# A new order table for the attention, its constants in another order, and TensorE products of the identity at launch and in gaps

## The chip, the cores and the metric

The kernel runs on one core of one Trainium2 chip. The metric is the device time of one execution in microseconds (us), lower is better. Engines: TensorE (PE; its weight loads are listed as PEld), VectorE (DVE), ScalarE (ACT), GpSimd (POOL) and SyncE (SP), which here issues almost all DMAs. Each engine works through its own queue in order and waits on semaphores of the others.

## The reference

An attention with a bias that depends on positions, then two gated feed-forward blocks; all in float32.

```
# q, k, v: (2 batches, 8 heads, 576 positions, 64); hidden = 32
scores = q @ k^T / 8
x    = log1p(|i - j|) / log1p(max(i, 1))
bias = relu(x * w1 + b1) @ w2                 # one table per head
attn = softmax(scores + bias);  a = attn @ v  # (1152 rows, 512)
h = a @ w_in;  g = h * clip(h + 3, 0, 6) / 6;  x = g @ w_out     # 2048 wide
xn = rmsnorm(x) * rms_g
out = (silu(xn @ w_gate) * (xn @ w_val)) @ w_out2                # 1536 wide
```

## The kernel before, in words

**Bias.** The bias of position i is needed for all distances. It is made in 36 groups of 16 positions, four tiles each. For each of the four tiles, one engine makes R (L346 to L356): the table T of log1p(distance), scaled once by w1 (L557), is cut off at a value of the row, NB1 on VectorE or SC on ScalarE (both from the norm table and b1, L558 and L559). START (for the first eight groups) and MID (for the others, in turn) say which engine makes each of the four. Four products with W2b on TensorE (`bias_mm`, token B.n) sum over the hidden units. The result is copied out of PSUM in two parts, scaled by INV (`bias_evac`), and stored to DRAM (`biasd`, L398) in a layout from which a load with another pitch (`bias<-biasd`, L424) reads the sheared bias of 128 query rows. Five such tables, one for each block c of query rows, are written; the first needed is c = 2 (groups 16 to 23). A load of bias waits for all stores of its table.

**Attention.** There are nine tiles of 128 query rows, and four pairs of heads in each: 36 units u. For unit u, token S.u is the scores (L439) into two PSUM buffers, of which there are only two in all. VectorE adds the bias and takes the maximum (L452, once for each head; a second small instruction reads the maximum). ScalarE takes the exponential (L463). TensorE transposes the 9 blocks (T.u.0 with four, T.u.1 with four, T.u.2 with one that holds columns of both heads) into three PSUM buffers shared with the bias products, VectorE or ScalarE copies them out (`et`, L483; ET says which), and PV.u multiplies with v (L501). Keys and queries are loaded (L295, L290, L283) and transposed (kT, qT; copies to kS and q). Raw key blocks have three buffers, so the load of a later block waits until an earlier one was transposed. Every four units the row sums are turned (rps) and copied (rt, L525) and the result is scaled.

**Order.** Each step has a key, a number from PARAMS. Steps with a key below `man` are written out by key for all engines. After that, TensorE follows ORDER, the table of tokens, word for word, while a scheduler places the other engines' instructions and the DMAs. TensorE's queue is in order: a token that waits holds all that follow. SP's queue of DMAs is in order too.

**Feed-forward.** From L713 on, products of split float32 (three passes each, `first` L720 and `second` L765), with weights loaded and split on the way (L124 to L165). The first eight weights are loaded and split during the attention.

Of the kernel before, what the change touches and what calls it, by code (L numbers as in the profile page):

```python
# [18 lines left out]
def shape_tables():  # L19
# [19 lines left out]
ORDER = """
kT.0,0,0 B.16 B.17 B.23 B.20 B.13 B.22 S.0 B.18 kT.0,1,0 B.12 B.9 kT.0,2,0 B.11 qT.0 B.19 B.10 kT.0,0,1 B.8 B.21 qT.1  # L40
kT.0,1,1 kT.1,0,1 T.0.2 S.1 B.14 T.0.0 S.2 kT.1,0,0 T.0.1 T.1.1 S.3 kT.1,1,0 S.4 T.1.2 T.2.2 kT.1,1,1 T.1.0 B.15 T.2.1
T.2.0 PV.0 B.24 B.26 T.3.2 PV.1 S.5 PV.2 T.4.1 T.3.0 B.25 qT.2 rps.0 T.3.1 T.4.0 B.27 T.5.0 T.4.2 S.6 B.28 PV.3 S.7
PV.4 T.5.2 T.5.1 T.6.2 S.8 T.7.0 T.6.1 PV.5 qT.3 T.6.0 S.9 PV.6 T.7.2 B.29 B.30 T.8.0 rps.1 T.8.2 T.7.1 S.10 T.8.1
B.32 B.31 PV.7 T.9.0 T.9.2 S.11 T.10.2 PV.8 T.10.0 B.33 T.9.1 S.12 qT.4 T.10.1 T.11.2 S.13 PV.9 B.35 T.12.0 T.11.0
B.34 PV.10 T.11.1 T.12.2 S.14 PV.11 B.0 rps.2 T.13.0 T.13.1 T.12.1 S.15 T.13.2 T.14.0 B.2 B.1 PV.12 T.14.2 T.14.1 S.16
PV.13 B.3 T.15.0 T.16.0 B.4 qT.5 S.17 T.15.2 T.15.1 rps.3 T.16.2 S.18 B.5 PV.15 PV.14 T.17.1 T.16.1 T.17.0 T.17.2 S.19
T.18.0 B.7 PV.16 PV.17 T.19.0 T.18.2 B.6 S.20 qT.6 T.19.1 T.19.2 S.21 T.18.1 T.20.0 rps.4 S.22 T.20.1 T.20.2 PV.18
PV.19 T.21.2 T.21.0 S.23 PV.20 T.21.1 T.22.1 T.22.0 S.24 PV.21 T.22.2 qT.7 T.23.0 S.25 T.23.2 T.24.2 T.24.0 T.23.1
rps.5 S.26 PV.22 PV.23 T.24.1 S.27 T.25.0 T.26.0 T.25.1 T.25.2 PV.24 S.28 T.26.2 T.27.1 qT.8 T.27.2 S.29 PV.25 T.27.0
rps.6 T.26.1 T.28.0 T.28.2 S.30 PV.26 PV.27 T.29.2 T.28.1 T.29.0 S.31 T.30.2 T.30.0 T.29.1 PV.28 T.31.0 S.32 PV.29  # L50
T.30.1 T.31.2 T.31.1 rps.7 PV.31 T.32.2 T.32.1 S.33 PV.30 T.32.0 S.34 T.33.0 T.33.2 T.33.1 S.35 PV.32 T.34.0 T.34.2
# [13 lines left out]
def kernel(ctx, tc, q, k, v, w1, b1, w2, w_in, w_out, w_gate, w_val, w_out2, rms_g, dtab, ntab, itab, out):  # L65
    nc = tc.nc
    B, H, S, D = q.shape
# [168 lines left out]
    if True:  # L236
# [48 lines left out]
        def load_k(b, blk, hh):  # L285

            if blk == 2:
                a = rawp.tile([128, H, D], F32, tag="rawk", name="rawk", bufs=BUFS["rawk"])
                for o in range(2):
                    nc.sync.dma_start(out=a[64 * o:64 * o + 64], in_=rows(k[o, :, 512:576, :]))  # L290
            else:
                a = rawp.tile([128, 2, 4, D], F32, tag="rawk", name="rawk", bufs=BUFS["rawk"])
                for c in range(2):
                    r0 = 256 * blk + 128 * c
                    nc.sync.dma_start(out=a[:, c], in_=rows(k[b, 4 * hh:4 * hh + 4, r0:r0 + 128, :]))  # L295
                a = a.rearrange("p c h d -> p (c h) d")
            raw_t["k", b, blk, hh] = a
# [187 lines left out]
        pv_t = {}  # L485
# [61 lines left out]
        nc.sync.dma_start(out=w2s, in_=w2)  # L547
        load_k(0, 0, 0)
        load_k(0, 1, 0)
        nc.sync.dma_start(out=INV, in_=itab.rearrange("g (o t) -> g o t", o=1).to_broadcast([16, 8, NG]))  # L550

        nc.vector.memset(nb1, 0.0)
        nc.scalar.activation(out=nb1, in_=nb1, func=ACTF.Exp)
        make_identity(nc, ident)
        nc.gpsimd.memset(W2b, 0.0)

        nc.vector.tensor_scalar_mul(T, T, w1c)  # L557
        nc.vector.tensor_scalar(out=NB1, in0=SC, scalar1=b1c, scalar2=-1.0, op0=ALU.mult, op1=ALU.mult)  # L558
        nc.vector.tensor_scalar_mul(SC, SC, b1c)  # L559
# [372 lines left out]
```

## Time and profile before

| what | value |
|---|---|
| median of the runs (three) | 640.93 us (640.75 to 642.7) |
| the profiled execution, its own time | 641.35 us |
| its span, first to last instruction | 639.5 us |
| TensorE busy | 617.6 us, 97% |
| VectorE, ScalarE, GpSimd busy | 442.9, 356.8, 143.6 us |
| chain that ended last, by engine | PE 91%, DMA 3%, DVE 3%, ACT 2% |

The span is what the trace covers; times of rows are counted from its start. A busy share over the whole span hides where an engine idles, so rows are read by stretch. In a row of the trace, "[2.11 <-X]" is the engine's idle time before the row, and what ended it.

### The profile page before, as it was taken

To read this page: it belongs to the slowest core of one execution; us is meant where nothing else is said; L and a number is where in the kernel's file an instruction comes from. 1 tells how busy PE (TensorE), PEld (TensorE's weight loads), DVE (VectorE), ACT (ScalarE), POOL (GpSimd) and SP (SyncE) were. 2 spreads that over 40 slices of the span, in tenths; PEclk is the share of its full clock that TensorE was granted. 3 is DMA by queue.
4 is the path that set the end of the run, shared out by engine and by line. 5 is a ranking of instruction groups with operands and counts; after the bars stand their busy time and mean duration, and the time that the engine had idled before them with its cause. 6 is when DMAs were issued, how large, how long until landed. Compare 5 with 4: busy or idle time off the path is not lost.

```text
span 639.5 us, 10867 instructions
## 1 busy us (share of the span) xinstructions
PE 617.6 (97%) x4136; PEld 520.1 (81%) x4136; DVE 442.9 (69%) x813; ACT 356.8 (56%) x730; POOL 143.6 (22%) x114
## 2 busy tenths in 40 slices
PE   5779999999999999999999999999999999999997
PEld 2246656667878999999999899999899999999996
DVE  5476796647555999888824799979677761387812
ACT  5879888968756555555425455563544331254411
POOL 1000110022110443333300133423323330032400
PEclk9989999999999999999999999999999999999999
DMA  7999867448100343433410133433424340054301
GB/s 161 248 297 266 245 207 209 131 103 205 62 2 1 120 145 133 130 116 120 130 33 1 58 99 121 152 99 118 146 100 132 119 145 2 33 197 135 98 1 49
DMA packets 73953, 77.78 MB, mean 122 GB/s; under 512 B 31917, under 2 KB 58669, under 8 KB 73901
## 3 DMA queue, kind: packets, MB, share of 16 engines
q1 hardware_dynamic: 73636, 77.02, 40.8%
q8 instruction: 32, 0.52, 0.3%
q14 instruction: 21, 0.16, 0.1%
q10 hardware_dynamic: 264, 0.07, 0.0%
HBM read 63.83 MB, written 13.25 MB: 121 GB/s over the span
## 4 chain that ended last, share of the span: by engine, by line
PE 91%; DMA 3%; DVE 3%; ACT 2%; issue 0%; ACTq 0%; SPq 0%; DVEq 0%
PE h L720 39%; PE ya L765 18%; PE yb L765 9%; PE s L439 7%; PE pv L501 7%; PE tps L100 6%; PE bps L369 4%; DVE R L356 1%; DMA biasd<-ev 1%; DMA bias<-biasd 1%; DMA raw<-in_moe_w_out_dram 1%; DMA b1c<-in_b_dram 1%; DVE e L452 1%; PE xnT L100 1%; ACT ev L392 1%; ACT e L463 1%
## 5 line engine op out<-in xcount | busy, mean ns | idle before, releaser
L165 POOL TENSOR_TENSOR wl<-wm,wh 128x512 fp32r<-128x512 f32 x85 | 125.9, 1481 | 302.3 <-ACT wh L136 181.9
L157 DVE SCALAR_TENSOR_TENSOR wm<-raw,wm 128x512 int32<-128x512 int32 x85 | 121.6, 1430 | 1.0
L729 ACT CAST gh<-r 128x384 fp32r<-128x384 f32 x84 | 43.2, 514 | 115.5 <-DVE r L752 68.7
L720 PE MATMUL h<-nh,wh 128*128 128x384 f32 x288 | 97.2, 338 | 0.0
L720 PE MATMUL h<-nh,wl 128*128 128x384 f32 x288 | 96.7, 336 | 0.0
L720 PE MATMUL h<-nl,wh 128*128 128x384 f32 x288 | 96.5, 335 | 0.0
L452 DVE CUSTOM_DVE_ANT_0 e<-s,bias 128x576 f32<-128x576 f32 x72 | 52.0, 754 | 28.1 <-PE s L439 20.1
L720 PE MATMUL h<-xh,wh 128*128 128x384 f32 x192 | 65.4, 340 | 0.0
L720 PE MATMUL h<-xh,wl 128*128 128x384 f32 x192 | 64.7, 337 | 0.0
L720 PE MATMUL h<-xl,wh 128*128 128x384 f32 x192 | 64.5, 336 | 0.0
L463 ACT ACTIVATE e<-e,m 128x576 f32<-128x576 f32 x72 | 55.6, 774 | 14.8 <-DVE m L452 14.6
L752 DVE TENSOR_TENSOR r<-r,h 128x384 f32<-128x384 f32 x36 | 19.9, 551 | 63.3 <-PE h L720 63.3
L153 DVE SCALAR_TENSOR_TENSOR wm<-raw,wm 128x512 int32<-128x512 int32 x85 | 58.9, 693 | 2.8
L732 DVE TENSOR_TENSOR gl<-r,gh 128x384 fp32r<-128x384 f32 x84 | 46.5, 554 | 16.8 <-ACT gh L729 16.8
L144 ACT ACTIVATE wm<-raw 128x512 f32<-128x512 f32 x85 | 57.0, 672 | 2.0 <-DMA raw<-in_moe_w_in_dram 1.5
L720 PEld LDWEIGHTS h<-nh,wh 128*128 128x128 f32 x288 | 54.1, 188 | 2.3 <-DVE nl L829 0.9
L720 PEld LDWEIGHTS h<-nl,wh 128*128 128x128 f32 x288 | 54.1, 188 | 1.4
L720 PEld LDWEIGHTS h<-nh,wl 128*128 128x128 f32 x288 | 54.0, 188 | 0.0
L748 ACT ACTIVATE r<-h 128x384 f32<-128x384 f32 x36 | 17.7, 492 | 64.9 <-PE h L720 64.9
L740 ACT ACTIVATE r<-h,half_c 128x384 f32<-128x384 f32 x48 | 27.7, 577 | 47.0 <-PE h L720 46.8
L136 ACT CAST wh<-wm 128x512 fp32r<-128x512 f32 x85 | 52.3, 616 | 0.9 <-DVE wm L157 0.8
L100 PE MATMUL tps<-ident,e 128*128 128x128 f32 x324 | 48.5, 284 | 2.6 <-DVE R L356 2.1
(95 smaller groups left out, 1101.3 us busy)
## 6 DMA issues: line engine op xcount, KB each, us to landing
raw<-in_moe_w_out_dram SPq DMA_DIRECT2D x33, 512.0 KB, 3.6
biasd<-ev SPq DMA_DIRECT2D x36, 295.5 KB, 4.0
raw<-in_moe_w_in_dram SPq DMA_DIRECT2D x18, 512.0 KB, 3.6
raw<-in_moe_w_gate_dram SPq DMA_DIRECT2D x18, 512.0 KB, 3.5
bias<-biasd SPq DMA_DIRECT2D x15, 576.0 KB, 5.6
raw<-in_moe_w_val_dram SPq DMA_DIRECT2D x16, 512.0 KB, 3.5
bias<-biasd SPq DMA_DIRECT2D x10, 288.0 KB, 5.1
rawk<-in_k_dram SPq DMA_DIRECT2D x18, 128.0 KB, 4.6
```

The lines of the kernel that those rows point to most:

```text
L100: nc.tensor.transpose(out, in_, ident[:n, :n])
L136: nc.scalar.copy(out=hi, in_=m)
L144: nc.scalar.activation(out=m, in_=raw[:, :, 1].bitcast(F32), func=ACTF.Abs, scale=2.0 ** -112)
L153: nc.vector.scalar_tensor_tensor(out=m, in0=raw[:, :, 0], scalar=29, in1=m, op0=ALU.logical_shift_right, op1=ALU.bitwise_or,)
L157: nc.vector.scalar_tensor_tensor(out=m, in0=raw[:, :, 1], scalar=-0x80000000, in1=m, op0=ALU.bitwise_and, op1=ALU.bitwise_or,)
L165: nc.gpsimd.tensor_tensor(out=lo, in0=m, in1=hi, op=ALU.subtract)
L439: nc.tensor.matmul(ps_of["s", u, a][sl, z, :SH], lhsT=q_t[t][half, p, sl], rhs=kS[b][half, p, z * SH:z * SH + SH], start=True, stop=True,)
L452: nc.vector.tensor_tensor_reduce(out=e_t[u][:, a, :].rearrange("p (z j) -> p z j", z=2), in0=s[:, :, :SH], in1=bt[u][:, a, :].rearrange("p ...
L463: nc.scalar.activation(out=e_t[u][:, a, :], in_=e_t[u][:, a, :], func=ACTF.Exp, scale=-1.0, bias=m_t[t][:, h:h + 1], accum_out=sum_t[t][:, ...
L720: nc.tensor.matmul(ps, lhsT=w[wz][:, c * 128:(c + 1) * 128], rhs=x[xz][:, c, :], start=(i == 0), stop=(i == 11),)
L732: nc.vector.tensor_tensor(out=gl, in0=g, in1=gh, op=ALU.subtract)
L765: nc.tensor.matmul(y_t[ph, n, t], lhsT=g[gz][:, t * 128:(t + 1) * 128], rhs=w[wz], start=(f == 0 and i == 0), stop=(f == F - 1 and i == 2),)
```

## The change

The table ORDER, the numbers in PARAMS and the engine strings are new. The constants stand in a block whose order is kept as written, with the loads of b1 and of the norm table exchanged and T scaled ahead of NB1 (in before, the scheduler placed T last). TensorE multiplies the identity by itself: EARLY = 10 times at launch, and twice for each token W, but only while no product with v is being gathered (`pv_t` is empty); that leaves eight of the W tokens with work, 16 products. These results are read by nobody. The last line of the table is shown in the diff; its starts are shown as rows below.

```diff
-    g0=-6.008, gs=0.583, g8=-0.495, gt=-0.138, g14=1.165, gr=1.195, man=-0.96, zra=-1.638, zrd=-0.49, zrp=-1.321,
+    g0=-5.852, gs=0.6, g8=-0.055, gt=-0.219, g14=1.366, gr=1.195, man=-0.96, zra=-1.514, zrd=-0.574, zrp=-2.014,
...
 ORDER = """
...
-T.34.1 PV.33 T.35.2 T.35.1 T.35.0 PV.34 PV.35 rps.8
+T.32.1 T.33.1 S.35 T.34.1 T.33.2 PV.32 PV.33 T.35.1 T.34.2 T.35.0 T.34.0 rps.8 T.35.2 PV.35 PV.34
...
-START = ["DAAA", "DDDD", "DDDD", "DDDD", "DDDD", "DDAA", "DDDD", "DDDD"]
-MID = ["DDAA", "DDDA"]
-ET = ["DADA", "DAAA", "ADAD"]
+START = ["DAAA", "DDDA", "DDDA", "DDDD", "DDDA", "DDDA", "DDDD", "DDDD"]
+MID = ["DDDD", "DDDA"]
+ET = ["DAAA", "AAAD", "DDAD"]
 KE = ["D", "A"]
-RB, RT, XH, XL = "PAAP"
+RB, RT, XH, XL = "PDAP"
+EARLY = 10
...
-        nc.sync.dma_start(out=T, in_=dtab.to_broadcast([128, S]))
-        nc.scalar.dma_start(out=SC, in_=ntab.rearrange("g (o t) -> g o t", o=1).to_broadcast([4, 32, 4 * NG]))
-        nc.sync.dma_start(out=w1c, in_=w1.rearrange("o (k z) -> o k z", z=1).to_broadcast([4, 32, 1]))
-        nc.scalar.dma_start(out=b1c, in_=b1.rearrange("(o k z) -> o k z", o=1, z=1).to_broadcast([4, 32, 1]))
...
+        warm_t = ps_v.tile([128, 4, 128], F32, tag="v", name="warm")
+
+        def warm(n):
+
+            if not pv_t:
+                for z in range(n):
+                    nc.tensor.matmul(warm_t[:, z % 4, :], lhsT=ident, rhs=ident, start=True, stop=True)
+
+        with tc.manual_schedule():
+            nc.sync.dma_start(out=T, in_=dtab.to_broadcast([128, S]))
+            nc.scalar.dma_start(out=b1c, in_=b1.rearrange("(o k z) -> o k z", o=1, z=1).to_broadcast([4, 32, 1]))
+            nc.sync.dma_start(out=w1c, in_=w1.rearrange("o (k z) -> o k z", z=1).to_broadcast([4, 32, 1]))
+            nc.scalar.dma_start(out=SC, in_=ntab.rearrange("g (o t) -> g o t", o=1).to_broadcast([4, 32, 4 * NG]))
...
+            make_identity(nc, ident)
+            nc.gpsimd.memset(W2b, 0.0)
+            warm(EARLY)
+
+            nc.vector.tensor_scalar_mul(T, T, w1c)
+            nc.vector.tensor_scalar(out=NB1, in0=SC, scalar1=b1c, scalar2=-1.0, op0=ALU.mult, op1=ALU.mult)
+            nc.vector.tensor_scalar_mul(SC, SC, b1c)
...
+        for i in range(ORDER.split().count("W")):
+            at(P["man"] + .001 * i, ("W", i), (), warm, 2)
```

Loads and stores on SP's queue, from the query loads to the first bias table's fourth store (rawk, rawq and vs are loads of keys, queries and values; biasd_72 is the first table). Before:

```order
L283 DMA rawq<-in_q_dram 128x8x64 x2
L398 DMA biasd_72<-ev 16x8x591
L304 DMA vs_138<-in_v_dram 128x4x64
L398 DMA biasd_72<-ev 16x8x591 x2
L304 DMA vs_138<-in_v_dram 128x4x64
L398 DMA biasd_72<-ev 16x8x591
```

With the change:

```order
L284 DMA rawq<-in_q_dram 128x8x64 x2
L305 DMA vs_138<-in_v_dram 128x4x64 x2
L399 DMA biasd_72<-ev 16x8x591 x2
L296 DMA rawk<-in_k_dram 128x4x64 x2
L399 DMA biasd_72<-ev 16x8x591 x3
```

Both value loads stand ahead of the first store, and two key loads follow the second store.

TensorE's queue from the second to the third scores (kps, qps and tps are transpositions of keys, queries and exponentials; s is scores; bps is a bias product; kS_136 is the first batch). Before:

```order
L100 MATMUL tps<-ident,e 128x128
L439 MATMUL s<-kS_136,q 128x288 x4
L369 MATMUL bps<-R,W2b 32x352 x4
L100 MATMUL tps<-ident,e 128x128 x4
L439 MATMUL s<-kS_136,q 128x288 x4
```

With the change:

```order
L550 MATMUL warm<-ident 128x128 x2
L440 MATMUL s<-kS_136,q 128x288 x4
L101 MATMUL qps<-ident,rawq 128x128 x4
L550 MATMUL warm<-ident 128x128 x2
L101 MATMUL kps<-ident,rawk 128x128 x4
L101 MATMUL tps<-ident,e 128x128 x4
L440 MATMUL s<-kS_136,q 128x288 x4
L370 MATMUL bps<-R,W2b 32x352 x4
L101 MATMUL tps<-ident,e 128x128
```

The single transposition now stands behind the third scores, and a key block stands ahead of them.

## Rows read from the trace of the kernel before

**Rows 1.** Busy time by stretch: start:end, length, then each engine, clock, DMA share, GB/s.

```profile
6.29:28.40 22.11, 17.82 (x126) 6.52 (x128) 15.99 (x48) 17.27 (x37) 0.94 (x3) 1.00 0.91 220
28.40:45.55 17.15, 12.96 (x86) 7.31 (x80) 11.79 (x31) 15.75 (x37) 0.00 (x0) 0.90 1.04 297
45.55:203.49 157.94, 155.53 (x1699) 109.67 (x1700) 102.38 (x267) 125.15 (x281) 19.24 (x19) 1.00 0.53 148
203.49:639.50 436.01, 431.31 (x2235) 396.59 (x2233) 311.88 (x465) 197.15 (x375) 122.06 (x82) 1.00 0.32 100
```

**Rows 2.** The chain of waits up to 46 us: start, length, what.

```profile
1.92 4.01 DMA b1c<-in_b_dram
...
23.44 4.88 DMA biasd<-ev
...
28.80 4.61 DMA bias<-biasd
...
33.43 0.76 DVE e L452
...
44.89 0.61 DVE kS L328
```

**Rows 3.** TensorE's timeline from 5 to 60 us: start, length, instructions.

```profile
11.45 1.24 PE L369 MATMUL bps<-R,W2b 128*32 128x304 f32 x8 [0.52 <-DVE R L356]
...
13.76 0.74 PE L369 MATMUL bps<-R,W2b 128*32 128x320 f32 x8
...
35.15 0.33 PE L100 MATMUL tps<-ident,e 128*128 128x128 f32 x1 [2.11 <-DVE R L356]
35.41 1.24 PE L439 MATMUL s<-kS,q 64*128 64x288 f32 x8
36.58 1.40 PE L369 MATMUL bps<-R,W2b 128*32 128x352 f32 x8
37.92 1.12 PE L100 MATMUL tps<-ident,e 128*128 128x128 f32 x4
38.96 1.71 PE L439 MATMUL s<-kS,q 64*128 64x288 f32 x8
...
45.55 1.24 PE L439 MATMUL s<-kS,q 64*128 64x288 f32 x8 [1.51 <-DVE kS L328]
...
47.43 0.66 PE L100 MATMUL tps<-ident,e 128*128 128x128 f32 x4
48.02 0.77 PE L369 MATMUL bps<-R,W2b 128*32 128x336 f32 x8
```

**Rows 4.** Busy time, clock and DMA share of three stretches of the start.

```profile
11.00:13.00 2.00, 1.55 (x11) 0.61 (x12) 1.54 (x7) 1.89 (x5) 0.00 (x0) 1.00 0.63 104
17.00:28.40 11.40, 8.50 (x62) 2.89 (x64) 6.85 (x20) 9.76 (x22) 0.00 (x0) 1.00 0.97 247
36.54:39.96 3.42, 3.42 (x18) 1.76 (x18) 2.47 (x7) 2.92 (x7) 0.00 (x0) 0.50 1.06 382
```

**Rows 5.** Timeline of VectorE and ScalarE in the start.

```profile
6.57 0.52 DVE L557 TENSOR_SCALAR T<-T,w1c 128x576 f32<-128x576 f32 x1
7.12 3.30 DVE L356 TENSOR_SCALAR R<-T,NB 128x320 f32<-128x320 f32 x11
...
20.21 0.90 ACT L392 ACTIVATE ev<-bps,INV 128x384 f32<-128x384 f32 x2
```

**Rows 6.** Groups by line, 45.5 to 203.5 us: busy us, mean ns, idle before.

```profile
L356 DVE TENSOR_SCALAR R<-T,NB 128x464 f32<-128x464 f32 (+9 forms) x45 | 20.0, 483 | 2.7 <-PE bps L369 2.7
L351 ACT ACTIVATE R<-T,SC 128x464 f32<-128x464 f32 (+9 forms) x27 | 19.2, 722 | 2.0 <-PE bps L369 1.7
...
L525 ACT COPY rt<-rps 128x512 f32<-128x512 f32 x8 | 4.7, 583 | 0.0
```

**Rows 7.** DMAs issued from 30 to 31.2 us: count, size, us to landing.

```profile
rawk<-in_k_dram SPq DMA_DIRECT2D x2, 128.0 KB, 5.6
```

**Rows 8.** Busy time from 80 to 100 us, columns as in rows 1.

```profile
80.00:100.00 20.00, 19.09 (x187) 11.92 (x185) 17.64 (x46) 18.01 (x38) 2.20 (x2) 1.00 0.70 217
```

More of the change, by code (lines that the diff above doesn't have):

```diff
@@ L35 @@
-    s1=0.381, d0=0.283, d1=0.659, e0=1.229, e1=1.572, t0=1.992, t1=1.874, t2=1.793, c0=0.767, c1=0.741, c2=-0.187,
-    pv=2.753, ri=0.666, rb=1.589, rps=2.464, rt=2.688, xf=4.008, xh=3.849, xl=6.122, w=-1.238, ws=0.454,
+    g0=-5.852, gs=0.6, g8=-0.055, gt=-0.219, g14=1.366, gr=1.195, man=-0.96, zra=-1.514, zrd=-0.574, zrp=-2.014,
+    zb=0.389, zev=0.606, zst=0.242, zevd=-77.57, zkt=-1.502, zkc=0.515, zqh=0.013, rd=0.043, ra=-0.14, rp=0.984,
+    b=0.797, ev=0.585, st=0.199, evd=82.888, k0=-3.654, k1=-2.479, k2=-1.384, k3=0.945, k4=-1.449, k5=1.246,
@@ L37 @@
+    k6=2.631, k7=0.548, k8=2.384, lk=-2.568, cc=-5.65, kt=0.704, kc=1.109, lv0=0.392, lv1=2.201, q0=-2.821,
+    q1=-1.81, q2=0.751, q3=7.178, lq1=-0.846, lq=-0.087, qa=-0.228, qb=3.664, qh=1.617, bl=-3.437, s0=-1.729,
+    s1=-1.484, d0=-0.955, d1=0.283, e0=1.585, e1=2.049, t0=1.219, t1=2.062, t2=1.036, c0=1.547, c1=0.355, c2=-1.385,
+    pv=2.443, ri=2.136, rb=2.68, rps=-1.667, rt=3.899, xf=4.961, xh=3.289, xl=6.492, w=1.517, ws=0.491,
 )
 ORDER = """
-kT.0,0,0 B.16 B.17 B.23 B.20 B.13 B.22 S.0 B.18 kT.0,1,0 B.12 B.9 kT.0,2,0 B.11 qT.0 B.19 B.10 kT.0,0,1 B.8 B.21 qT.1
@@ L41 @@
[L41 to L50, printed above, removed]
@@ L51 @@
-T.30.1 T.31.2 T.31.1 rps.7 PV.31 T.32.2 T.32.1 S.33 PV.30 T.32.0 S.34 T.33.0 T.33.2 T.33.1 S.35 PV.32 T.34.0 T.34.2
-T.34.1 PV.33 T.35.2 T.35.1 T.35.0 PV.34 PV.35 rps.8
-"""
-START = ["DAAA", "DDDD", "DDDD", "DDDD", "DDDD", "DDAA", "DDDD", "DDDD"]
-MID = ["DDAA", "DDDA"]
-ET = ["DADA", "DAAA", "ADAD"]
+B.13 B.23 B.22 S.0 B.11 B.10 B.19 kT.0,0,0 B.20 qT.0 B.8 B.9 kT.0,1,0 B.16 B.21 W kT.0,0,1 W W kT.0,2,0 kT.1,0,1 B.12
+W kT.0,1,1 W B.17 S.1 qT.1 W kT.1,0,0 T.0.0 B.18 S.2 B.14 T.0.2 W T.1.2 T.0.1 S.3 kT.1,1,0 W kT.1,1,1 T.1.1 S.4 T.2.2
@@ new lines @@
+T.2.0 B.15 PV.0 T.3.0 W T.2.1 B.24 W B.26 PV.2 W W T.3.2 T.1.0 rps.0 B.25 W S.5 PV.1 T.3.1 W W T.4.2 S.6 W W T.4.0 W W
+qT.2 T.4.1 PV.3 S.7 B.27 T.5.2 W T.5.0 B.28 B.29 T.5.1 S.8 T.6.2 T.6.0 T.6.1 PV.4 S.9 rps.1 T.7.2 PV.5 T.8.2 T.7.1
+T.7.0 B.30 PV.6 T.8.0 T.9.0 S.10 qT.3 T.8.1 B.31 B.32 PV.7 T.9.1 S.11 PV.8 B.33 T.9.2 T.10.0 T.10.1 T.11.2 B.34 B.35
+T.11.1 T.11.0 T.10.2 S.12 PV.10 S.13 PV.9 T.12.0 T.12.2 S.14 T.12.1 rps.2 qT.4 S.15 T.13.1 B.2 T.13.0 qT.5 PV.11
+T.14.2 S.16 T.15.2 T.13.2 T.14.1 PV.12 B.1 B.0 PV.13 T.14.0 T.16.0 S.18 T.15.0 T.15.1 B.3 B.4 B.5 S.17 PV.15 PV.14
@@ new lines @@
+S.19 T.16.2 T.17.0 rps.3 T.17.1 T.16.1 T.18.0 T.18.2 PV.16 T.17.2 B.6 B.7 T.19.0 T.18.1 S.20 T.19.2 rps.4 qT.6 PV.17
+S.21 T.19.1 T.20.0 S.22 T.20.2 T.20.1 PV.19 PV.18 T.21.1 S.23 PV.20 S.24 T.21.2 T.21.0 T.22.1 T.22.0 T.23.1 rps.5
+T.23.2 S.25 T.22.2 T.24.0 qT.7 PV.21 T.24.1 S.26 T.24.2 T.23.0 T.25.0 T.25.2 PV.22 S.27 T.25.1 PV.23 T.26.2 S.28 PV.24
+PV.25 T.26.0 T.27.2 rps.6 T.27.0 T.26.1 S.30 T.28.0 T.27.1 qT.8 S.29 PV.27 PV.26 T.29.2 S.31 T.30.2 T.29.1 T.28.2
+T.28.1 T.29.0 T.30.0 T.30.1 S.32 PV.28 T.31.0 T.31.2 T.31.1 S.33 PV.30 PV.31 T.32.0 T.32.2 rps.7 S.34 PV.29 T.33.0
@@ L539, in x_part @@
                 copy(engine)(out=h_, in_=xf_t[t])
-        nc.sync.dma_start(out=T, in_=dtab.to_broadcast([128, S]))
-        nc.scalar.dma_start(out=SC, in_=ntab.rearrange("g (o t) -> g o t", o=1).to_broadcast([4, 32, 4 * NG]))
-        nc.sync.dma_start(out=w1c, in_=w1.rearrange("o (k z) -> o k z", z=1).to_broadcast([4, 32, 1]))
-        nc.scalar.dma_start(out=b1c, in_=b1.rearrange("(o k z) -> o k z", o=1, z=1).to_broadcast([4, 32, 1]))
[L547 to L559, printed above, removed]
+        warm_t = ps_v.tile([128, 4, 128], F32, tag="v", name="warm")
[8 more added lines that the diff above has]
+            nc.scalar.dma_start(out=SC, in_=ntab.rearrange("g (o t) -> g o t", o=1).to_broadcast([4, 32, 4 * NG]))
+            nc.sync.dma_start(out=w2s, in_=w2)
+            load_k(0, 0, 0)
+            load_k(0, 1, 0)
+            nc.sync.dma_start(out=INV, in_=itab.rearrange("g (o t) -> g o t", o=1).to_broadcast([16, 8, NG]))
+            nc.vector.memset(nb1, 0.0)
+            nc.scalar.activation(out=nb1, in_=nb1, func=ACTF.Exp)
+            make_identity(nc, ident)
[4 more added lines that the diff above has]
+            nc.vector.tensor_scalar_mul(SC, SC, b1c)
         def bias_consts():
@@ L667 @@
         line = [tuple(int(y) if y.lstrip("-").isdigit() else y for y in z.split(".")) for z in ORDER.split()]
+        line = [("W", line[:i].count(("W",))) if z == ("W",) else z for i, z in enumerate(line)]
         turn_of = {z: i for i, z in enumerate(line)}
@@ L670 @@
         todo = sorted(plan, key=lambda z: z[:2])
-        assert sorted(turn_of) == sorted(short(z[2]) for z in todo if z[2][0] in ("S", "T", "PV", "B", "kT", "qT", "rps")), "table"
+        assert sorted(turn_of) == sorted(short(z[2]) for z in todo if z[2][0] in ("S", "T", "PV", "B", "kT", "qT", "rps", "W")), "table"
         done = set()
```

4 lines of the change are left out of this document (removed).

## The prediction

> **What bounds the kernel now.** I read the stages first: time, engine busy time and clock of each stretch [rows 1]. From 203.49 us on, the feed-forward part keeps TensorE busy for 431 of 436 us, and the change leaves the order of every engine there as it was. From 45.55 to 203.49 TensorE is busy for 155.5 of 157.9 us. So almost all idle time that could be won lies before 45.55: 22.11 - 17.82 = 4.3 us and 17.15 - 12.96 = 4.2 us, and the 6.29 us before the first useful matrix work. Then I read what the start waits for. The chain of waits [rows 2] goes through the store of the last block of the first bias table (issued 23.44, 4.88 us), the load of the sheared bias (issued 28.80, 4.61 us), and at the end a copy of keys (44.89). TensorE's own rows [rows 3] show two more losses. Before about 12.6 us and between 36.54 and 39.96 its pieces take nearly twice their usual time: a bias product of 304 columns takes 1.24 us at 11.45, one of 320 columns 0.74 us at 13.76. For the second stretch the clock column says 0.50 [rows 4]; for the first it says 1.00, so there only the durations tell. And at 35.15 the queue's head is a single transposition (part 2 of unit 0) that needs both exponentials of unit 0. The scores of unit 1 stand behind it until 35.41, though the buffers that they write are free once VectorE has read them, at 33.43 + 0.77 = 34.20 [rows 2].
>
> **The change part by part.** The base is the profiled execution (641.35 us, 0.42 above the median of the runs, 640.93).
>
> *Constants.* VectorE now scales T before it needs the other two constants; today T (0.52 us) is scaled last, and the R tiles start at 7.12 [rows 5]. T can be scaled while the last small load is under way (b1 landed at 1.92 + 4.01 = 5.93 [rows 2]). The noise table's load now stands second on ScalarE's queue. If it lands as late as b1 did, the R tiles start 0.5 us sooner; if it is 0.5 us later than that, nothing is won. I take 0.5.
>
> *Ten products at launch.* The trace holds no 128-column product of the whole array; the nearest rows give bounds. Four transpositions of 128 columns take 0.66 us at 47.43, so 0.17 each; four score products of 288 columns take 1.24 us, 0.31 each [rows 3]. I take 0.25, twice that at half clock: ten take 5 us, from about 1.6 us, where nothing else is ready; even at 0.62 they end at 7.8, about when the first product's last R tile is there (7.12 + 3 ScalarE tiles). Their use is the clock. A bias product at full clock is 0.5 us shorter (1.24 against 0.74). On the way to the last store that counts about once, since later products wait for ScalarE's copies, not for the array: 0.5 us.
>
> *The way to the first bias load.* ScalarE copied the last block of the first table out at 20.21 to 21.11 [rows 5]; with the two gains it ends near 20.1. The store left only at 23.44, since SP was still issuing key loads and earlier stores. The new order sends two value loads ahead of the first store, instead of between stores, and the DMA engines have room there: a share of 0.63 between 11 and 13 us, 0.97 from 17 to 28.4 [rows 4]. I let the store and so the bias come 1.7 us sooner: 1.0 from above, 0.7 from SP's shorter backlog. Bounds: 0 (the DMA engines are full) and 3 (a store right after its copy). In the DMA page of the Trainium skill (DMA: Bandwidth & Descriptors, section "Queues, rings and completion order") each engine consumes a ring's descriptors in order, so the two loads would delay the first store by their own time. Here that is 256 KB at 247 GB/s, 1.04 us, of which the room of 0.37 x 2 us covers 0.74: by this rule the sum would be 0.3 us smaller.
>
> *Scores of unit 1 before the transpositions of unit 0.* They follow VectorE's second reading directly: 34.2 - 1.7 = 32.5, not 35.41. That VectorE is free rests on its R tiles for two more groups being done by then; ScalarE gives up work here, not VectorE, so this is the thinnest cover.
>
> *The next keys.* The new order has the keys of the other batch (kT.1,0,0) ahead of the transpositions of unit 0 and the scores of unit 2. Their load may start only when the array has turned an earlier block, near 29.5; today's key loads of 30.0 to 31.2 us landed 5.6 us after their issue [rows 7], and 29.5 + 5.6 is 35.1. I take 35.0. So unit 2's scores start near 35.0 + 0.6 (keys) + 0.6 (four transpositions) = 36.2, less what overlaps, say 35.9; today 38.96. From there to unit 4's scores: scores 1.2, one bias product 0.75, a warm pair 0.5, six transpositions 0.9 gives 39.25; scores of unit 3 1.25, then two key blocks 1.2, a warm pair 0.5, four transpositions 0.6, which is 42.8. VectorE's path, two readings of 0.76 and the key copy of 0.61, ends at 42.6. So unit 4 starts at **42.8**, not 45.55: **-2.75 us**. At that point the new order has done one key block (0.5) and one transposition (0.13) more: **-0.63**. Of the sixteen products in gaps, twelve lie before waits for the bias or the keys and cost nothing; without that wait they would cost 3.0. The four others are in the walk.
>
> *ScalarE to VectorE.* Between 45.5 and 203.5 ScalarE made 27 R tiles [rows 6]; about 10 stay. 17 x 0.72 = 12.3 us leave ScalarE and 17 x 0.48 = 8.2 us come to VectorE. The nine copies rt (0.58 on ScalarE [rows 6]) move to VectorE, at about its price of a 512-column copy, the key copy of 0.61: +5.5. Nine large et copies go the other way, and nine of a quarter of the columns come back, which I estimate at half the price: -5.5 + 2.7. VectorE goes from 102 to about 113 of 158 us, ScalarE from 125 to 111. TensorE loses only 2.4 us to waits here now. I take **0**, with 1.2 either way.
>
> *End of attention.* The last small transposition now stands directly ahead of the product that needs it, so TensorE waits for its copy (a 128-column one, again half of 0.61, and the hand-overs): **+0.5**.
>
> Sum: -2.75 - 0.63 + 0 + 0.5 = **-2.9**: 638.45 for the profiled execution and 638.0 against the median. I write 638.1.
>
> **Rivals.**
> *Full DMA engines.* The bias lands no sooner. Share 0.97 to 28.4 [rows 4] speaks for it, 0.63 at 11 against it. Unit 1's scores then start at 34.2, unit 2's near 37.0, unit 4's at 43.7: -1.85 - 0.63 + 0.5 = -2.0, so 638.9.
>
> *The clock falls in the wait for the bias.* Today it fell after TensorE had idled from 33.0 to 35.15, and four pieces paid: 1.40 against 0.77 for a bias product, 1.12 against 0.66 for four transpositions, 1.71 against 1.24 for scores [rows 3], together 1.56 us. The warm pairs run before the new wait, not in it, so TensorE may idle there for two microseconds as well. My walk has no such stretch; with it, 639.6. In the Trainium skill (TensorE: Matmul & The Clock Gate, section "Part 4: PE-mode transpose") transpositions do not count as a busy array in the same way, which speaks for this rival, as this stretch is rich in them. The rows show only that they run at full speed once the clock is up.
>
> *VectorE becomes the bound (slower).* From 80 to 100 us it is already busy for 17.64 of 20 us [rows 8], and some 11 us of work are added to the middle. If a third of it falls there, 21.3 us do not fit in 20, and every reading of scores comes late. The kernel is slower by more than 0.3% if TensorE waits for over 2.9 + 1.9 = 4.8 of the 11 us; at half of the 11 the time is 643.5. Against it: ScalarE, the busier of the two, is relieved, and R tiles can be made early.
>
> *The change does little.* If TensorE's waits only move past 45.55, 640.9.
>
> **How the numbers follow.** 0.3%, about what a measurement of this kernel tells from no change, is 1.9 us: faster is below 639.0, slower above 642.85. Chances: my walk 0.50; full DMA engines 0.14 (638.9, half on either side of the border); the clock 0.14 and little change 0.10 (both within 0.3%); VectorE 0.12. So faster 0.57, same 0.31, slower 0.12. Range: unit 4 starts at 41.25 if the keys land at 33.5, and the middle gains 1.2: 635.4. It starts at 44.9 if both the DMA and the clock go against me, and the middle loses 1.2: 641.4. The walk alone: 636.8 to 639.4.
>
> **What would show it.** Right: full-speed products from the first one on (0.74, not 1.24), the first bias load issued before 27.5, scores of unit 1 right after VectorE's second reading, no stretch at 0.50 before 46, unit 4's scores by 43. Wrong: a wait of TensorE for VectorE between 60 and 140 us above 2 us, a load of bias at 28 or later, a second clock stretch, or a long wait at the key block of the other batch.

## The result and the profile after

The changed kernel takes 636.24 us (median of six runs, 633.32 to 638.27), the kernel before, timed beside it, 642.22 us. The ratio is 0.9898, with a 95% interval of 0.9868 to 0.9927: about 1% faster. The profiled execution took 636.64 us with a span of 634.9 us, where before had 641.35 and 639.5. The runs differ by TensorE's mean granted clock: two with 1.000 took 633.32 and 634.50 us, four with 0.996 or 0.997 took 636.19 to 638.27. Line numbers of the changed kernel are 1 higher than before in the attention and 14 higher in the feed-forward part.

Busy time by stretch, changed kernel, in the columns of [rows 1]. The first row runs from unit 4's scores to the first feed-forward product (called the middle here), the second from there to the end:

```profile
43.64:198.71 155.07, 152.94 (x1694) 108.84 (x1694) 111.58 (x293) 114.64 (x256) 18.91 (x19) 1.00 0.55 156
198.71:634.90 436.19, 431.38 (x2234) 396.62 (x2232) 311.94 (x465) 196.69 (x374) 122.00 (x82) 1.00 0.32 100
80.00:100.00 20.00, 18.84 (x204) 12.41 (x202) 19.35 (x52) 14.51 (x31) 1.97 (x2) 1.00 0.71 206
8.22:11.63 3.41, 3.41 (x16) 1.45 (x18) 2.41 (x10) 2.92 (x8) 0.00 (x0) 0.50 0.94 202
```

Against [rows 1]: unit 4's scores start at 43.64 instead of 45.55 (-1.91), the middle is 155.07 us long instead of 157.94 (-2.87), the feed-forward stretch 436.19 instead of 436.01 (+0.18). Together that is the span's -4.6. The last row is a stretch at half clock right at the start, after a first rise. In before the first pieces, up to about 12.6 us, took half-clock times too [rows 3], though its clock column does not say so.

TensorE's timeline, changed kernel (start, length, instructions, idle time before and what ended it; a float32 product leaves two records, so x20 are ten products):

```profile
1.56 4.03 PE L550 MATMUL warm<-ident 128*128 128x128 f32 x20 [1.56 <-POOL ident masks.py:199]
8.08 2.38 PE L370 MATMUL bps<-R,W2b 128*32 128x320 f32 x8 [2.49 <-DVE R L357]
10.40 1.12 PE L101 MATMUL kps<-ident,rawk 128*128 128x128 f32 x4
11.44 1.29 PE L370 MATMUL bps<-R,W2b 128*32 128x304 f32 x16
...
31.77 0.75 PE L440 MATMUL s<-kS,q 64*128 64x288 f32 x2
33.54 1.23 PE L440 MATMUL s<-kS,q 64*128 64x288 f32 x6 [1.02 <-DVE m L453]
...
35.64 0.60 PE L101 MATMUL kps<-ident,rawk 128*128 128x128 f32 x4
...
36.61 1.47 PE L440 MATMUL s<-kS,q 64*128 64x288 f32 x8
...
43.64 1.24 PE L440 MATMUL s<-kS,q 64*128 64x288 f32 x8 [0.32 <-DVE kS L329]
...
196.11 0.27 PE L101 MATMUL tps<-ident,e 128*128 128x128 f32 x1
196.31 1.09 PE L502 MATMUL pv<-et,vs 128*64 128x128 f32 x16
197.25 0.44 PE L502 MATMUL pv<-et,v 128*64 128x128 f32 x4
```

The launch products end at 5.59. TensorE then waits 2.49 us for the first R tiles, the clock falls (8.22 to 11.63, above), and the first bias product and key block run at half speed; a key block takes 1.12 us there and 0.60 at 35.64. Compared with [rows 3], the scores of unit 1 begin at 31.77 instead of 35.41, but all except the first product stand until 33.54; unit 2 is at 36.61 (38.96).

VectorE's timeline, changed kernel, against [rows 5] and the reading at 33.43 in [rows 2]:

```profile
5.62 0.52 DVE L568 TENSOR_SCALAR T<-T,w1c 128x576 f32<-128x576 f32 x1 [4.10 <-DMA w1c<-in_w_dram]
7.01 0.29 DVE L569 TENSOR_SCALAR NB<-SC,b1c 128x144 f32<-128x144 f32 x1 [0.88 <-DMA rawk<-in_k_dram]
...
7.55 3.00 DVE L357 TENSOR_SCALAR R<-T,NB 128x320 f32<-128x320 f32 x10
...
30.12 0.76 DVE L453 CUSTOM_DVE_ANT_0 e<-s,bias 128x576 f32<-128x576 f32 x1 [2.38 <-DMA bias<-biasd]
...
32.72 0.76 DVE L453 CUSTOM_DVE_ANT_0 e<-s,bias 128x576 f32<-128x576 f32 x1 [1.83 <-DMA bias<-biasd]
```

T is scaled 0.95 us sooner, but NB stands until 7.01 and the R tiles start at 7.55, 0.43 later than before. The idle time at 7.01 is put down to a key load that landed in the same moment; NB reads SC and b1c, no keys. SP's own waits before 14 us (engine, line, what it waited for, us in total, times, longest) point to the load that was late, whose landing itself is not in the trace:

```profile
SPq L291 <- DMA SC<-in_ntab_dram: 0.5, 1, 0.5
```

The chain of waits of the changed kernel (start, length, what), against [rows 2]:

```profile
22.80 3.57 DMA biasd<-ev
26.85 5.84 DMA bias<-biasd
32.72 0.76 DVE e L453
```

The last store of the first table leaves 0.64 us sooner and lands 1.31 us faster, so the load follows 1.95 sooner. But that load takes 5.84 us instead of 4.61: VectorE's first reading gains 1.9 us (30.12 against 32.05 in before's timeline), the second only 0.71.

Groups by line, changed kernel, 43.64 to 198.71, against [rows 6]:

```profile
L357 DVE TENSOR_SCALAR R<-T,NB 128x464 f32<-128x464 f32 (+9 forms) x63 | 27.0, 477 | 3.4 <-PE bps L370 3.3
L526 DVE COPY rt<-rps 128x512 f32<-128x512 f32 x9 | 6.2, 685 | 1.8 <-PE rps L101 1.6
L352 ACT ACTIVATE R<-T,SC 128x448 f32<-128x448 f32 (+8 forms) x9 | 6.6, 730 | 1.5 <-PE bps L370 1.5
```

### The profile page after: what moved, and what is told of

Same layout as the page of the kernel before. It is cut to its first block, busy times and chain, and to the rows that moved or that the text cites. A ratio compares the mean times of both kernels' runs of the same rounds, so it can differ in the third digit from the quotient of the medians.

```text
span 634.9 us, 10967 instructions
## 1 busy us (share of the span) xinstructions
PE 621.3 (98%) x4188; PEld 527.3 (83%) x4188; DVE 454.4 (72%) x848; ACT 341.2 (54%) x695; POOL 143.2 (23%) x114
## 4 chain that ended last, share of the span: by engine, by line
PE 89%; ACT 3%; DMA 3%; DVE 2%; SPq 1%; issue 1%; DVEq 0%; ACTq 0%
PE h L734 40%; PE ya L779 18%; PE yb L779 9%; PE pv L502 6%; PE s L440 6%; PE tps L101 5%; PE bps L370 3%; ACT ev L393 1%; ACT e L464 1%; DMA bias<-biasd 1%; DMA raw<-in_moe_w_out_dram 1%; DVE e L453 1%; PE xnT L101 1%; ACT et L484 1%; PE rps L101 1%
## 5 line engine op out<-in xcount | busy, mean ns | idle before, releaser
L440 PE MATMUL s<-kS,q 64*128 64x288 f32 (+1 forms) x320 | 48.6, 427 | 1.7 <-DVE m L453 1.0
```

The lines of the kernel that those rows point to most:

```text
L440: nc.tensor.matmul(ps_of["s", u, a][sl, z, :SH], lhsT=q_t[t][half, p, sl], rhs=kS[b][half, p, z * SH:z * SH + SH], start=True, stop=True,)
```

## The experiments

Times are medians; ratios are to the kernel before, timed on the same chip (641.59, 641.88 and 642.13 us in the three groups of runs). The changed kernel is called "after" here.

**1. The two small loads exchanged** (a_load_swap): of after's constants, the norm table's load goes first on ScalarE's queue and b1 second. SP's order of DMAs is the same as in after.

```diff
  nc.sync.dma_start(out=T, in_=dtab...)
+ nc.scalar.dma_start(out=SC, in_=ntab...)
- nc.scalar.dma_start(out=b1c, in_=b1...)
  nc.sync.dma_start(out=w1c, in_=w1...)
- nc.scalar.dma_start(out=SC, in_=ntab...)
+ nc.scalar.dma_start(out=b1c, in_=b1...)
```

> The changed kernel with the two small loads on ScalarE's queue exchanged back (norm table first, then b1), T still scaled first. In the changed kernel the norm table landed at about 6.9 us and the R tiles started at 7.55, not at 6.6. Theory 1 (the load that stands second sets the start, and the larger one costs more there): NB1 at about 6.0, R tiles from about 6.6; the first bias load 0.5 to 1.0 us sooner, and up to 0.9 us of it at the end: 635.3 to 636.2. Rival (the DMA engines and SP's queue set the bias load): R tiles sooner, bias load and end as in the changed kernel, 636.2.

Measured: 634.92 us, ratio 0.9889 (0.9871 to 0.9908). VectorE's timeline of this kernel:

```profile
5.99 0.29 DVE L569 TENSOR_SCALAR NB<-SC,b1c 128x144 f32<-128x144 f32 x1
...
6.53 3.00 DVE L357 TENSOR_SCALAR R<-T,NB 128x320 f32<-128x320 f32 x10
```

And TensorE's:

```profile
1.56 3.96 PE L550 MATMUL warm<-ident 128*128 128x128 f32 x20 [1.56 <-POOL ident masks.py:199]
7.05 1.84 PE L370 MATMUL bps<-R,W2b 128*32 128x320 f32 x8 [1.53 <-POOL W2b L574]
8.82 0.66 PE L101 MATMUL kps<-ident,rawk 128*128 128x128 f32 x4
9.41 1.23 PE L370 MATMUL bps<-R,W2b 128*32 128x304 f32 x16
...
41.85 1.24 PE L440 MATMUL s<-kS,q 64*128 64x288 f32 x8
```

NB no longer waits, the R tiles start 1.02 us sooner than in after, TensorE idles for 1.53 us instead of 2.49, and the key block at 8.82 runs at full speed. From the start of the first bias product to the end of the second, 3.59 us pass (7.05 to 10.64) instead of 4.65 (8.08 to 12.73). Sooner start and kept clock, 1.03 + 1.06 = 2.09 us, are what arrives in this execution, the fastest of the five: the chain's last store of the first table leaves at 20.75 instead of 22.80, and unit 4's scores start 1.79 us sooner.

The sooner start is the work of the load order: in the traces of the three kernels with the exchange the R tiles start at 6.53 to 6.73, in the eight with after's order at 7.33 to 7.56. The kept clock is not shown to be. Experiment 8 has after's loads and table up to unit 4's scores, and R tiles at 7.54, yet its clock stayed up; experiment 6 has the exchange, and its first key block ran at half speed. So the changed kernel's own load order lost about 1 us at launch; the second microsecond goes with the clock. Whether the first reaches unit 4's scores is open: with the clock up they start at 41.85 here and at 41.58 in experiment 8. The medians, 634.92 and 636.24, point the same way, with 634.92 below the first theory's range; their intervals overlap.

**2. The same without the launch products** (a_load_swap_no_launch), and **3. after without them** (a_only_gaps):

```diff
# 2
-EARLY = 10
+EARLY = 0
# 3
-            if not pv_t:
+            if not pv_t and n != EARLY:
```

In both the scheduler also puts the two value loads behind the first store.

> The changed kernel with its two small constant loads exchanged (634.92 us), now without the ten launch products; the products in gaps stay. The scheduler then puts the two value loads behind the first store instead of ahead of it. Theory 1: what the exchange opened up is the clock that stays up from the launch products on: without them the bias products before about 12.5 us take 1.2 to 1.9 us at half speed again, the first bias load is issued at 26 or later instead of 24.84, and the time is 636 to 637.5. Theory 2: the exchange works through the earlier R tiles alone, and the clock adds nothing: the bias load is issued before 25.5, and the time is 634.3 to 635.5.

> The changed kernel without the ten products at launch, with the sixteen in gaps. Without any product the kernel lost 0.5% of its gain, and its profile had a stretch at clock 0.50 from 34.47 to 37.88. Theory 1 (the products in gaps keep the clock up before unit 1's scores; those at launch are spent before work comes): no stretch at 0.50 between 25 and 45 us, and 636 to 637, ratio 0.990 to 0.992. Rival (the launch products do it): 638 to 639, ratio 0.995, as without any.

Measured: 637.22 us (0.9917, 0.9902 to 0.9933) and 637.57 (0.993, 0.9915 to 0.9945). TensorE's timeline of the former:

```profile
7.26 2.38 PE L370 MATMUL bps<-R,W2b 128*32 128x320 f32 x8 [7.26 <-POOL W2b L574]
9.57 1.12 PE L101 MATMUL kps<-ident,rawk 128*128 128x128 f32 x4
10.62 1.85 PE L370 MATMUL bps<-R,W2b 128*32 128x304 f32 x16
```

The three lengths (2.38, 1.12, 1.85) are those of half clock (1.84, 0.66 and 1.23 in experiment 1), the first bias load leaves at 27.04, and the time lies in the range of experiment 2's first theory: it holds, the exchange alone doesn't carry the gain. In 3 the clock stays up from 28 to 46 us, as its first theory says, but the time lies above that theory's range. The ratios compare each kernel with before on its own chip. By them the exchange of the loads is worth 0.8 us without launch products (0.993 to 0.9917) and 0.6 with them (0.9898 to 0.9889); the products are worth 2.1 us in after and 1.8 with the exchange. All four pairs of intervals overlap, so that the two help each other is not shown. Nor is it all clock: the value loads moved too, and the middle of both kernels without launch products is longer (157.01 and 156.78 us).

**4. Twenty launch products** (a_early20): in after, to fill the wait.

```diff
-EARLY = 10
+EARLY = 20
```

> The changed kernel with 20 instead of 10 products at launch. In its profile the ten ended at 5.6, TensorE idled to 8.08, and the clock, up at 4.80, fell from 8.21 to 11.63, in which the first bias product took 2.4 us and four key transpositions 1.1 us. Theory 1 (the gap after the launch products throws the clock away): with twenty TensorE is busy to about 7.6, no stretch at 0.50 after the first rise, the first group copied out about 1 us sooner and the end 0.5 to 1.0 us sooner, 635.3 to 635.8. Rival (ScalarE's copies and the DMAs hide it): the clock stays up and the end is the same.

Measured: 636.81 us (0.9919, 0.9904 to 0.9934), no gain over after; the first theory's range was 635.3 to 635.8. The wait for the first R tiles is gone and the clock stays up there, but the scheduler now sends five loads of values ahead of the first store, which leaves at 12.90 instead of 11.43. ScalarE's timeline:

```profile
16.42 0.90 ACT L393 ACTIVATE ev<-bps,INV 128x336 f32<-128x336 f32 x2 [1.88 <-DMA biasd<-ev]
```

And TensorE's:

```profile
7.86 1.84 PE L370 MATMUL bps<-R,W2b 128*32 128x320 f32 x8 [0.16 <-DVE R L357]
...
17.38 1.88 PE L370 MATMUL bps<-R,W2b 128*32 128x352 f32 x16 [2.13 <-ACT ev L393]
19.20 2.29 PE L440 MATMUL s<-kS,q 64*128 64x288 f32 x8
```

ScalarE's copy waits 1.88 us for a buffer that an earlier store has not yet read, TensorE then waits 2.13 us, and the clock falls there instead (scores of 2.29 us instead of 1.24).

**5. No identity products at all** (a_no_warm): the loop in `warm` never runs. **6. Experiment 1 without the products in gaps** (a_load_swap_no_gaps):

```diff
# 5
-            if not pv_t:
+            if False:
# 6
-            if not pv_t:
+            if not pv_t and n == EARLY:
```

> The changed kernel without its 26 identity products (nothing else differs). Theory 1 (the gain is in the order and in the relief of ScalarE): the ten at launch bought nothing, since the clock was up at 4.80 and down again at 8.21 before real work came; without them the first products still run at half clock to about 12 us. The sixteen in gaps stand before waits. So within 0.7 us of the changed kernel's 636.2 (ratio to before 0.989 to 0.991). If a stretch at clock 0.50 comes back between 30 and 41 us, it costs up to 1.6 us: 637.8. Rival (the identity products are the gain, through the clock): most of the 6 us is lost, 640 or more.

> The changed kernel with its two small constant loads exchanged (634.92 us), now without the sixteen products in gaps; the ten at launch stay. Theory 1: they keep the clock up through the waits for the bias and the keys: without them there is a stretch at half clock between 28 and 45 us, and the time is 635.6 to 637.3. Theory 2: with the constants sooner no wait is long enough for the clock to fall, and the products only take room in TensorE's queue: no stretch at half clock, and the time is 633.8 to 635.2.

Measured: 638.77 us (0.9949, 0.993 to 0.9967), and 634.79 (0.9882, 0.9868 to 0.9897). Busy time and clock of a stretch of the former, in the columns of [rows 1]:

```profile
34.47:37.88 3.41, 2.91 (x13) 2.22 (x12) 0.98 (x4) 1.98 (x5) 0.00 (x0) 0.50 1.00 326
```

TensorE's timeline of the latter:

```profile
9.52 1.12 PE L101 MATMUL kps<-ident,rawk 128*128 128x128 f32 x4
...
32.09 1.23 PE L440 MATMUL s<-kS,q 64*128 64x288 f32 x6 [0.81 <-DVE m L453]
...
42.17 0.66 PE L101 MATMUL tps<-ident,e 128*128 128x128 f32 x4 [1.21 <-DVE kS L329]
```

Without any identity products a half-clock stretch like that of before comes back. The time of 5 lies between its two theories, and it is not the price of the clock alone, since the value loads stand behind the first store there, as in 2 and 3. Experiments 3 and 5 differ in the sixteen products in gaps alone (and, by that, in the place of two transfers on SP's queue): with them there is no such stretch, and the times, 637.57 and 638.77, point to a gain that the intervals do not separate from none. With the bias as soon as in experiment 1 the stretch does not come back (experiment 6), though TensorE waits up to 1.21 us, and the sixteen products make no measurable difference. What they are for is the case in which the bias is late.

**7. The one swap of tokens in the old kernel** (b_swap): S.1 ahead of T.0.2 in before's table, nothing else.

```diff
-T.0.2 S.1
+S.1 T.0.2
```

> The kernel before with two neighbouring tokens exchanged: the scores of unit 1 ahead of the single transposition of unit 0. Theory 1: the scores start near 34.2 instead of 35.4 and unit 4's near 44.5 instead of 45.55: 1.0 us faster, ratio 0.998 to 0.999. If the idle time is shorter than before, the stretch at clock 0.50 may go as well: then up to 2.6 us, ratio 0.996. Rival (unit 4's scores wait for keys whose load and copy do not move): no change, unit 4 at 45.5.

Measured: 640.60 us, ratio 0.9988 (0.9973 to 1.0003). TensorE's timeline:

```profile
32.99 1.26 PE L439 MATMUL s<-kS,q 64*128 64x288 f32 x8
34.88 0.33 PE L100 MATMUL tps<-ident,e 128*128 128x128 f32 x1 [0.63 <-ACT e L463]
...
43.99 1.24 PE L439 MATMUL s<-kS,q 64*128 64x288 f32 x8 [1.64 <-DVE kS L328]
```

Busy time and clock of its start, in the columns of [rows 1]:

```profile
10.97:45.55 34.58, 26.39 (x201) 12.40 (x198) 23.54 (x67) 30.52 (x70) 0.48 (x1) 1.00 0.99 267
```

The swap moves unit 1's scores to 32.99 and unit 4's by 1.56 us, and the half-clock stretch is gone without a single identity product; a bias load that left at 27.58 in this execution, 0.8 sooner, is part of it. The time stays at the first theory's 0.998 to 0.999; the 0.996 that it gave for a stretch that goes as well did not come. The clock stays up although waits of 0.63 to 1.64 us and many transpositions lie there. The Trainium skill (TensorE: Matmul & The Clock Gate, section "Part 4: PE-mode transpose") says that transpositions do not count as a busy array in the same way. This stretch shows no loss from that, but it holds bias products and scores too, so it does not refute the sentence. In the time the swap alone is not told from no change.

**8. The old middle** (a_old_middle): after's table up to S.4, then the remaining tokens in before's order, with after's keys and strings. **9. All old engine strings** (a_old_engines): after with START, MID, ET and RT of before. **10. MID alone of before** (a_old_mid). **11. ET and RT of before** (a_old_et_rt). **12. The new strings in the old kernel** (b_new_engines): before with START, MID, ET and RT of after.

```diff
 W kT.1,1,1 T.1.1 S.4
-T.2.2 T.2.0 B.15 PV.0 T.3.0 W T.2.1 B.24 W B.26 PV.2
+T.2.2 T.1.0 B.15 T.2.1 T.2.0 PV.0 B.24 B.26 T.3.2 PV.1 S.5 PV.2
...
-MID = ["DDDD", "DDDA"]
+MID = ["DDAA", "DDDA"]
-ET = ["DAAA", "AAAD", "DDAD"]
+ET = ["DADA", "DAAA", "ADAD"]
-RB, RT, XH, XL = "PDAP"
+RB, RT, XH, XL = "PAAP"
```

(8 takes the lines of tokens alone, which are broken anew here, 10 those of MID, 11 those of ET and RT, 9 all strings and START, 12 the reverse of 9 in before.)

> The changed kernel's table up to unit 4's scores, after that the remaining tokens in the order of before; new engine strings. Theory 1 (engine strings shorten the middle): unit 4's scores at 43.6 as in the changed kernel, the middle at 154.5 to 156, 635.5 to 637. Rival (the new order after unit 4 gives it): the middle at about 157.3, 638.4.

> The changed kernel with the engine strings START, MID, ET and RT of before. Theory 1 (17 R tiles and the rt copies moved from ScalarE to VectorE shorten the middle by 2.2 us): the time from unit 4's scores to the first feed-forward product goes from 155.1 back to about 157.3, and with some loss in the start the kernel takes 638.5 to 639.5. Rival (the order of the table gives the middle's gain): that time stays below 155.8 and the kernel within 0.7 us of 636.2.

> The changed kernel with MID alone as before (half of the later groups again with two R tiles on ScalarE, the other half with one). With all four engine strings of before the whole gain was lost: unit 4 at 46.2 instead of 43.6, and 158.8 instead of 155.1 us from there to the first feed-forward product. Theory 1 (R tiles are what overloads ScalarE): most of both comes with MID: unit 4 at 45 or later and the middle at 157 or more, 640 or more. Rival (the copies et and rt do it): the middle below 156 and the kernel within 1 us of 636.2.

> The changed kernel with ET and RT of before (who copies the transposed exponentials and the row sums out); START, MID, table and keys stay new. Theory 1: the middle became shorter because these two strings take copies off ScalarE and match the new table: the stretch from unit 4's scores to the first feed-forward product is 157 to 159 us instead of 155.07, and the time is 638.5 to 640.5. Theory 2: the table and the keys alone shortened the middle: the stretch stays within 0.7 of 155.1, and the time is 635.8 to 637.3.

> The kernel before with the four new engine strings (START, MID, ET, RT) alone; table, keys and constants stay old. Theory 1: the strings are worth something only with the table that was made for them: 641 to 646 us, with a middle of 157.5 us or more. Theory 2: the relief of ScalarE is a gain of its own: the middle is 155 to 156.5 us instead of 157.94 and the time 638.5 to 640.3.

| kernel | us | ratio (95%) | unit 4's scores at | middle, us |
|---|---|---|---|---|
| before | 642 | 1 | 45.55 | 157.94 |
| after | 636.24 | 0.9898 (0.9868 to 0.9927) | 43.64 | 155.07 |
| 8 old middle | 646.74 | 1.0072 (1.0054 to 1.009) | 41.58 | 166.06 |
| 9 all old strings | 641.89 | 1.0003 (0.9991 to 1.0015) | 46.16 | 158.76 |
| 10 old MID | 639.52 | 0.9947 (0.9926 to 0.9969) | 47.41 | 154.53 |
| 11 old ET, RT | 639.78 | 0.9966 (0.995 to 0.9982) | 43.23 | 159.70 |
| 12 new strings, old table | 642.19 | 1.0001 (0.9987 to 1.0015) | 44.56 | 159.60 |

The start of 8 is after's up to unit 4's scores. TensorE's timeline of it:

```profile
8.06 1.84 PE L370 MATMUL bps<-R,W2b 128*32 128x320 f32 x8 [1.87 <-DVE R L357]
9.83 0.66 PE L101 MATMUL kps<-ident,rawk 128*128 128x128 f32 x4
...
41.58 1.24 PE L440 MATMUL s<-kS,q 64*128 64x288 f32 x8
```

Its first bias product starts where after's does, but at full clock, and unit 4's scores follow 2.06 us sooner than in after. So in these two traces the clock of the first microseconds, which differs between executions, goes with a difference about as large as the whole gain of the start (1.91 us) that after's trace shows.

Busy time of 11 in its middle and from 80 to 100 us, in the columns of [rows 1]:

```profile
43.23:202.93 159.70, 154.21 (x1696) 109.24 (x1695) 109.86 (x283) 117.16 (x267) 19.11 (x19) 1.00 0.54 151
80.00:100.00 20.00, 17.73 (x198) 11.86 (x195) 19.87 (x52) 13.01 (x27) 1.98 (x2) 1.00 0.66 192
```

TensorE's longest waits in that middle (us in total, times, longest):

```profile
PE bps L370 <- DVE m L453: 2.2, 3, 1.1
PE tps L101 <- DVE et L484: 0.8, 3, 0.4
PE pv L502 <- DVE et L484: 0.8, 1, 0.8
```

In 11 the middle is 4.6 us longer than in after, a little more than the first theory's 157 to 159 us, and the time is within that theory's range. VectorE is busy for 19.87 of 20 us between 80 and 100 and TensorE for 17.73; in after they are at 19.35 and 18.84. That fits the new ET taking large copies from VectorE where the new MID has filled it. But the strings are no gain by themselves: in 12 the middle is longer than before's by 1.7 us, with waits for both engines' copies, as its first theory has it. And the new table is none with the old strings (9, where both theories left some of the gain), and the old order of the middle is worse than all with the new strings and keys (8: one wait for ScalarE's copies is 2.5 us, and the granted clock is 0.50 from 57.28 to 60.69 and from 81.17 to 84.58). Both expectations for 8 failed. 10 meets neither theory whole: unit 4 is 3.8 us later, as the first has it, while the middle is as short as in after, as the rival has it. MID works in the start. Its TensorE timeline:

```profile
36.26 0.84 PE L101 MATMUL kps<-ident,rawk 128*128 128x128 f32 x4 [0.93 <-DMA rawk<-in_k_dram]
37.89 0.66 PE L101 MATMUL tps<-ident,e 128*128 128x128 f32 x4 [0.78 <-ACT q L338]
```

The keys and ScalarE's copy of queries come late, and a second half-clock stretch follows (38.77 to 42.18). Its seven runs spread from 636.22 to 640.54 us, so the 3.8 us of one execution need not hold for all.

## Why the prediction was right, and where not

The direction was right and 636.24 lies inside the range; the point 638.1 was 1.9 us too slow. By its profiled execution the prediction took -2.9, and -4.7 came. That the point is this near is partly luck: it looked for nearly all of the gain in the start, which gave less, and for none in the work of the middle, which gave most. Of its signs, the first bias load before 27.5 came; full-speed products from the first one on, no half-clock stretch before 46 and unit 4's scores by 43 did not. Its terms:

*Constants: failed.* (What the prediction calls the noise table is the norm table.) The term said 0.5 us sooner; the R tiles came 0.43 later, beyond the bound of "nothing" that was set. The working assumed that the second load on ScalarE's queue lands as b1 did. By the wait of SP the norm table in that place came a microsecond later (SP's load that waited for it left at 6.93; b1 had landed at 5.93 [rows 2]). Experiment 1, which sets b1 second, is the term as it was meant: R tiles at 6.53, 0.59 before the 7.12 of before.

*Launch products: the mechanism right in part, the condition missed.* They can have the clock up for the first work, but do not in every execution. In the six traces without them the first key block takes 1.08 to 1.12 us; in the seven with ten of them it takes 0.66 in two (experiments 1 and 8) and 1.12 in five (after, 6, 9, 10, 11). The prediction let them run until about when the R tiles are there; they took 4.03 us, not 5, and the tiles were late. In after, 9, 10 and 11 a wait of 2.25 to 2.57 us follows them and the clock falls; in after this leaves the key block at half speed, so in this execution they gave next to nothing. The pattern "wait, then half clock" was read rightly, but looked for only at 35 us.

*First bias load: the time right, the reasons half.* Predicted 26.7 (28.39 in before, less 1.7), measured 26.45. The store did not leave 1.7 us sooner, though, but 0.64, and landed 1.31 faster. Part of it went again one step later: the load itself took 1.2 us longer. The DMA share during it was 0.97, 0.89 in before, which fits the rival of full DMA engines; no run tests it.

*Unit 1 to unit 4.* That the single transposition held unit 1's scores back was right (experiment 7: 2.4 us sooner at 32.99, of which 0.8 is the sooner bias load of that execution). Scores of unit 1 were predicted together at 32.5; the first product came at 31.77 and the rest at 33.54, for the second half of the bias. The next keys, on which the walk spent its longest wait, did not hold TensorE at 35.64. Unit 4 started at 43.64, not 42.8: -1.91 where -2.75 was taken. Unit 1's last products were 1.04 us late by the walk and unit 2 then 0.71 (36.61 for 35.9), which is most of the 0.84.

*The middle: the term of mis-sized cost.* The prediction took 0 for work from ScalarE to VectorE and +0.5 for the end, with 0.63 of work done sooner. That makes 157.94 - 0.63 + 0.5 = 157.81 us; 155.07 came, 2.74 less, beyond the 1.2 allowed. The amounts of work were right (R tiles on ScalarE 9 for "about 10", VectorE 111.6 us for 113, ScalarE 114.6 for 111; rt 0.685 us each for 0.61). Wrong was the reasoning from idle time: TensorE showed only 2.41 idle in the middle, so little seemed to be had. Its idle time fell by just 0.28 (2.41 to 2.13); the gain lies in what counts as busy. Taken record by record, from each start to the next and without idle time, TensorE goes from one kind of work (scores, bias, products with v, and transpositions of exponentials, keys, queries or row sums) to another 149 times in before's middle and 140 times in after's. These steps take 37.1 us together in before and 34.2 in after, all others 118.4 and 118.8. So the new table wins by putting more of one kind behind each other; two of the nine changes are those around the key block that moved into the start. The traces of the kernels with the old table (before, 7 and 12) have 149 changes and 37.1 to 37.5 us, those with the new one 140 and 34.1 to 34.6, whatever their strings and launch products. What the strings decide is idle time: 2.4 us in before but 3.9 in 12, and 2.1 in after but 4.9 in 9 and 5.5 in 11 (1.7 in 10, so the new MID is not what it needs there). That is why table and strings bring the gain only together. Idle time also differs between kernels that differ at launch alone (2.1 in after, 3.7 in 2), so smaller parts of the middle stay open.

*End of attention.* The transposition at 196.11 is followed by sixteen records of products that do not need it, and the product that does follows them at 197.25 without a wait; the +0.5 did not come.

*Rivals.* VectorE became nearly full (19.35 of 20 us), yet TensorE's waits for it between 60 and 140 us sum to 1.7 us, less than the 2 us that were set as the mark; in experiment 11, two strings away, the three shown there make 3.8 us in its whole middle. The clock rival's stretch came in experiments 5 and 10, not in the changed kernel, whose own stretch lies at launch; the price of 1.56 us adds up three pieces, not four.

## What to carry to other kernels

Filler work that is to keep the clock up helps only if the next work arrives before the clock falls: look at the end of the filler and at the row behind it, and then at which small load is late. The start of one trace is one draw: where the clock differs between executions, compare several traces with the same start before a change is given the credit. Where a table of order and a division of work between engines were made together, test them together: halves of such a change can each look useless. And little idle time on the busiest engine does not mean that nothing is to be won there: count how often it changes from one kind of work to another, and what such a step takes.

## What was not expected of the hardware

- Ten products of 128 columns took 4.03 us at launch, in after; most pairs in gaps (four records) took 0.61 us at full clock, 0.30 each, two pairs in a row 1.06, as against the 0.25 each that was estimated.
- With the same ten launch products, the key block after the first bias product took 0.66 us in the profiled execution of experiment 1, but 1.12 in that of experiment 6, where the ten took 4.64 us and TensorE idled for only 1.00 us behind them. In experiment 8 the ten took 4.63 us, TensorE idled for 1.87, and the key block took 0.66. So the products do not raise the clock in every execution; why is open.
- After's six runs are faster where the mean clock was 1.000. That mean does not tell the start, though: experiment 2's profiled execution has 1.000 and its first products at half speed, and its two slowest runs, 638.11 and 638.42 us, have 1.000 too.
- Which of two small loads goes first on ScalarE's queue decided about 1 us of the start of all R tiles (7.33 to 7.56 in eight traces, 6.53 to 6.73 in three).
